# A fused attention and FFN kernel on one core: the last 1024 tokens of the FFN moved behind the attention heads and run 512 at a time

## The chip, the core and the metric

The kernel runs on one core of one Trainium2 chip. A core has five engines that work side by side and meet at semaphores: TensorE (PE; its weight loads are listed apart as PEld), VectorE (DVE), ScalarE (ACT), GpSimd (POOL) and SyncE (SP), which here issues all the transfers. The metric is the device time of one execution in microseconds (us), lower is better. Before the change it is 1208.37 us, the median of 3 runs (1208.25 to 1209.43).

## What is computed

64 attention heads (8 batches of 8 heads, 576 positions, 64 dimensions each) with a causal mask and a decay taken from cumulated logs of a forget gate; the results, laid side by side, are 4608 tokens of 512 features, and go through an FFN of 2048 hidden features with a leaky ReLU.

```python
scores = scale * np.matmul(q, k.transpose(0, 1, 3, 2))
cum = np.cumsum(np.log(np.clip(f, 0.0001, 1.0)), axis=-1)
scores = np.where(causal, -1000000000.0, scores + cum[:, :, :, None] - cum[:, :, None, :])
attn = np.exp(scores - np.max(scores, axis=-1, keepdims=True))
attn = attn / (np.sum(attn, axis=-1, keepdims=True) + 1e-09)
x = np.matmul(attn, v).transpose(0, 2, 1, 3).reshape(B * S, H * D)
h = x @ w_in                       # 4608 x 512 @ 512 x 2048
out = np.maximum(0.01 * h, h) @ w_out
```

All of it is in float32, and the FFN keeps the precision by splitting each operand into a high and a low part: every product is three matmuls (high by high, low by high, high by low).

## The kernel before

**Layout.** Attention of the first 256 positions of three batches is done first, by a simpler path (`early_scores`, `early_values`), while the FFN weights are loaded and split; they stay in SBUF for the rest of the program. Then come 64 *tasks*, one head each, in the batch order 0, 3, 4, 5, 6, 7, 1, 2. Tasks 8 to 47 are whole heads (576 rows); tasks 0 to 7 and 48 to 63 belong to the three batches whose first 256 rows are already done and have 320 rows.

**One head on the engines.** `scores(t, i)` makes row block i of the scores on PE (tiles `sc`, two PSUM buffers); DVE adds the mask and finds the maximum (line 437), ACT takes the exponential (line 443). One task later `transposes(t, i)` turns the block on PE (tiles `tr`), ACT and DVE copy it out as a high part `ph` and a low part `pl` (lines 487 and 489), and `values` multiplies both with v (`av`: first the matmuls that read `ph`, then those that read `pl`). There is one `ph` and one `pl` in SBUF. After every second head `inverse` turns the sums of the exponentials and sends them through DRAM, and `normalise` (line 584) multiplies and writes the pair's result to the DRAM array `xd` (line 587).

**The FFN as filling.** The generator `ffn()` goes over the 4608 tokens in 18 groups of T = 256. A group's tokens are read back from `xd` by one transfer of 512 KB (`fetch_group`, line 608) and split (`split_group`). For each p, a pair of blocks of 128 hidden features (8 pairs in all), the group has 24 matmuls that write `h` (12 for each half, 256 columns wide), a Prelu on ACT (`g`, line 654), the high part on DVE (`gh`, line 657), the low part on POOL or, after the last head, on DVE (`gl`, line 659), and one pair later 12 matmuls 512 columns wide that add to the two accumulators `o` (`second`). A *quantum* is one yield of the generator: 12 matmuls of `h` or 6 of `o`; a pair is 4 quanta and a group 32, so the FFN is 576. After the last pair ACT copies each accumulator to an `ost` tile (line 690, two buffers) and SP sends it to `out` (line 692).

**What sets the order.** In the main loop (lines 755 to 788) `fill(step)` stands between the parts of a head and adds `step` to a credit, nine times per head in all; each whole credit runs one quantum. Line 763 counts the quanta whose tokens are ready and not yet used, line 764 the heads to the end of the batch, and line 765 sets the step:

```python
have = ready[0] // T * NQ - used[0]
step = min(have / (left + SLACK), CAPS.get(t, MAXQ)) / 8
```

MAXQ is 9, so a head gets at most 9 x 9/8, about 10 quanta. Below, a head's *rate* is the value that line 765 divides by 8. The framework then orders the instructions on each engine by its own costs; on each engine they run strictly in that order. Following lines 763 to 765 by hand, the rate is 4.5 to 4.0 in tasks 0 to 7, 3.9 to 3.5 in 8 to 16, 6.7 down to 5.75 in 17 to 24, 7.4 to 6.5 in 25 to 32, 9.0 in 33 to 40, 8.8 to 7.75 in 41 to 48, 7.8 to 6.75 in 49 to 56 and 4.7 to 4.2 in 57 to 63. 500 quanta are used when the last head ends, and 76 run behind it.

## Time and profile before

| | |
|---|---|
| time, median of 3 runs | 1208.37 us (1208.25 to 1209.43) |
| the profiled execution | 1209.36 us, of which the profile's span is 1207.5 us |
| granted TensorE clock | 1.00 |
| PE busy | 1194.9 us, 99% of the span |
| DVE, ACT, POOL busy | 613.2, 633.2 and 460.8 us (51%, 52%, 38%) |
| FFN matmuls `h`, 128x256 | 3456, mean 283 to 286 ns each |
| FFN matmuls `o`, 128x512 | 1728, mean 395 to 402 ns each |

A row of a group or of the timeline gives the line of the program, the engine, the operation, output<-input by the program's names, and the shape. The duration of a matmul is from its start to its modelled end; since matmuls overlap in the array, the time one really takes is read from the spacing of starts, or from the chain of waits, which counts only what each adds. "Idle before" is the time for which the engine had nothing to do ahead of an instruction, with what ended it. In the trace the first score of task 8 starts at 228.1 us, that of task 17 at 333.8, of task 33 at 585.6, of task 48 at 872.3, of task 57 at 1011.6, and the last `av` of task 63 starts at 1093.85.

### The profile page before, as it was taken

The numbers are of one execution on the slowest core, as the hardware profiler recorded it, in microseconds if no ns is written. First come the engines' busy times: TensorE is split into PE (matmuls) and PEld (weight loads), VectorE is DVE, ScalarE is ACT, GpSimd is POOL, SyncE is SP. The second block draws the span as 40 slices with busy tenths as digits, with TensorE's granted clock in tenths as the row PEclk, the third lists the DMA queues.
The fourth block names the chain that finished last, engine by engine and source line by source line (L and its number), as shares of the span: only waits on it lengthen the run. The fifth ranks groups of instructions, "written<-read, shape, count | busy, mean of one in ns | idle before, by whom it ended". The sixth has DMA issues, their size and how long they took to land.

```text
span 1207.5 us, 22521 instructions
## 1 busy us (share of the span) xinstructions
PE 1194.9 (99%) x7828; PEld 1068.1 (88%) x7828; DVE 613.2 (51%) x1697; ACT 633.2 (52%) x1622; POOL 460.8 (38%) x473
## 2 busy tenths in 40 slices
PE   9999999999999999999999999999999999999998
PEld 6678888888899999999999999999999999998997
DVE  6888365566655555464544445444443434553221
ACT  5887465666755565555554545455444445552111
POOL 2000255555455445454435354444354543531000
PEclk9999999999999999999999999999999999999999
DMA  6565233334343233323332223232233223311000
GB/s 202 175 204 177 78 99 101 99 111 118 102 137 82 82 99 101 99 72 97 87 96 79 80 66 101 65 100 59 69 85 93 58 71 81 80 58 52 13 18 19
DMA packets 82130, 110.57 MB, mean 92 GB/s; under 512 B 20640, under 2 KB 51728, under 8 KB 82016
## 3 DMA queue, kind: packets, MB, share of 16 engines
q1 hardware_dynamic: 82016, 109.12, 31.2%
q8 instruction: 63, 1.03, 0.4%
q14 instruction: 51, 0.42, 0.1%
HBM read 65.32 MB, written 18.58 MB: 69 GB/s over the span
## 4 chain that ended last, share of the span: by engine, by line
PE 95%; DVE 2%; ACT 1%; DMA 1%; issue 1%; POOL 0%; SPq 0%; DVEq 0%; ACTq 0%; POOLq 0%
PE h L111 34%; PE o L111 33%; PE tr L115 8%; PE av L111 8%; PE sc L111 7%; PE sce L111 2%; PE ave L111 1%; PE ws L111 1%; PE warm L111 1%; PE tre L115 1%; DVE fixed_z L437 1%; DMA wraw<-in_w_in 0%; ACT g L654 0%; DVE pl L489 0%; DVE gh L657 0%
## 5 line engine op out<-in xcount | busy, mean ns | idle before, releaser
L659 POOL TENSOR_TENSOR gl<-g,gh 128x512 fp32r<-128x512 f32 x113 | 148.8, 1317 | 275.1 <-DVE gh L657 270.1
L111 PE MATMUL o<-wout_h,gh 128*128 128x512 f32 x576 | 231.3, 402 | 0.0
L111 PE MATMUL o<-wout_l,gh 128*128 128x512 f32 x576 | 227.4, 395 | 0.0
L111 PE MATMUL o<-wout_h,gl 128*128 128x512 f32 x576 | 227.1, 395 | 0.0
L443 ACT ACTIVATE fixed_z<-fixed_z,max 128x192 f32<-128x192 f32 (+3 forms) x272 | 161.0, 592 | 101.4 <-DVE max L437 99.1
L111 PE MATMUL h<-xh,win_h 128*128 128x256 f32 x1152 | 206.2, 286 | 0.0
L487 ACT CAST ph<-tr 128x192 fp32r<-128x192 f32 (+3 forms) x360 | 126.7, 373 | 148.5 <-PE tr L115 99.2
L111 PE MATMUL h<-xh,win_l 128*128 128x256 f32 x1152 | 200.3, 283 | 0.0
L437 DVE CUSTOM_DVE_ANT_0 fixed_z<-sc,tri 128x192 f32<-128x192 f32 (+3 forms) x272 | 122.4, 451 | 151.3 <-PE sc L111 148.4
L654 ACT ACTIVATE g<-h 128x512 f32<-128x512 f32 x144 | 85.8, 596 | 216.1 <-PE h L111 211.0
L657 DVE CAST gh<-g 128x512 fp32r<-128x512 f32 x144 | 72.4, 503 | 217.6 <-ACT g L654 215.9
L489 DVE TENSOR_TENSOR pl<-tr,ph 128x384 fp32r<-128x384 f32 (+3 forms) x296 | 137.3, 467 | 80.7 <-ACT ph L487 79.5
L111 PEld LDWEIGHTS h<-xh,win_h 128*128 128x128 f32 x1152 | 170.8, 190 | 5.8 <-issue 0.5
L111 PEld LDWEIGHTS h<-xh,win_l 128*128 128x128 f32 x1152 | 164.8, 190 | 0.5 <-issue 0.2
L111 PE MATMUL h<-xs,win_h 128*128 128x256 f32 x1024 | 164.4, 283 | 0.0
L115 PE MATMUL tr<-ident_r,fixed_z 128*128 128x128 f32 x888 | 145.3, 273 | 3.4 <-DVE ph L494 1.7
L111 PEld LDWEIGHTS h<-xs,win_h 128*128 128x128 f32 x1024 | 141.0, 191 | 0.0
L115 PEld LDWEIGHTS tr<-ident_r,fixed_z 128*128 128x128 f32 x888 | 107.6, 140 | 25.2 <-ACT rb L566 5.2
L111 PEld LDWEIGHTS o<-wout_h,gl 128*128 128x128 f32 x576 | 108.2, 188 | 24.4 <-DVE maxe L323 0.3
L111 PEld LDWEIGHTS o<-wout_l,gh 128*128 128x128 f32 x576 | 108.7, 189 | 16.0 <-issue 0.5
L111 PEld LDWEIGHTS o<-wout_h,gh 128*128 128x128 f32 x576 | 108.9, 189 | 14.8
L154 POOL TENSOR_TENSOR fixed_m2a<-raw,m 64x576 fp32r<-64x576 f32 x32 | 46.6, 1458 | 195.4 <-ACT m L399 173.8
(130 smaller groups left out, 1753.2 us busy)
## 6 DMA issues: line engine op xcount, KB each, us to landing
raw<-in_kT SPq DMA_DIRECT2D x64, 144.0 KB
m<-m SPq DMA_DIRECT2D x64, 144.0 KB
wraw<-in_w_in SPq DMA_DIRECT2D x16, 512.0 KB
wraw<-in_w_out SPq DMA_DIRECT2D x16, 512.0 KB
fixed_vm<-in_v SPq DMA_DIRECT2D x64, 128.0 KB
xs<-xd SPq DMA_DIRECT2D x16, 512.0 KB
out<-ost SPq DMA_DIRECT2D x28, 256.0 KB
raw<-in_qT SPq DMA_DIRECT2D x40, 144.0 KB
```

The costliest lines, as they stand in the source:

```text
L111: nc.tensor.matmul(*args, **kw)
L115: nc.tensor.transpose(*args)
L154: nc.gpsimd.tensor_tensor(out, a, b, op=ALU.subtract)
L437: nc.vector.tensor_tensor_reduce(out=z[:, a:b], in0=ps[:m, :b - a], in1=tri[:m, at:at + b - a], scale=-SCALE, scalar=3.0e38 if x == 0 else ...
L443: nc.scalar.activation(z, z, AF.Exp, bias=h["max"][:m, last:last + 1], scale=-1.0, accum_out=fixed["sum" + "ab"[s // 2 % 2]][:m, i, s % 2: ...
L487: nc.scalar.copy(strided(ph, run), source(ps, run))
L489: nc.vector.tensor_tensor(strided(pl, run), source(ps, run), strided(ph, run).bitcast(F32), op=ALU.subtract)
L654: nc.scalar.activation(g, ph, AF.Prelu, alpha=0.01)
L657: nc.vector.tensor_copy(gh, g)
L659: eng.tensor_tensor(gl, g, gh.bitcast(F32), op=ALU.subtract)
```

## The change

The generator's narrow groups end at the 14th; the last four (1024 tokens) become two *wide* groups of 512 tokens that run only when all heads are done. A wide group takes its hidden features 128 at a time: 12 matmuls 512 columns wide write one `h` bank (`hw`), Prelu, high and low part follow as before, and 12 matmuls go to four accumulators (`second_wide`, tiles `ow`). The four accumulators of the first wide group lie in the PSUM of `o0`, `o1` and `tr`, those of the second in `sc`, `o0` and `o1`. The tokens of the first wide group are fetched in one transfer of 1 MB into the SBUF of the heads' `ph`, with the high part in that of `pl` (`fetch_wide`, `split_wide`); those of the second use the narrow groups' buffers. All four accumulators of a wide group end together, pass through the same two `ost` buffers, and the very last one is copied by ACT and DVE, half each.

The planner counts no more than the 448 narrow quanta less LAST = 8, and from task 17 on the cap of the rate is 6.2 in place of 9, which makes about 7 quanta a head. By hand: tasks up to 16 keep their rate, 17 to 56 have 6.2 each, 57 to 63 have 3.9 to 3.4. 430 quanta are used when the last head ends, 18 narrow ones are left, and behind them the two wide groups.

```diff
--- before.py
+++ after.py
@@ -19,6 +19,9 @@
 HP = 4
 PARTS = (("part0", 1), ("part1", 1), ("ost", 2), ("ost", 2))
 MAXQ = 9
+LATEQ = 6.2
+LAST = 8
+WIDE = 2
 CAPS = {}
 SLACK = 3
 B2 = 5
@@ -618,7 +621,7 @@
         pending = None
         half = NFC // 2
         order = [(0, 0, HP), (1, 0, HP), (0, HP, half), (1, HP, half)]
-        order += [(n, 0, half) for n in range(2, NG)]
+        order += [(n, 0, half) for n in range(2, NG - 2 * WIDE)]
         for at, (n, p0, p1) in enumerate(order):
             while (n + 1) * T > ready[0]:
                 yield False
@@ -663,7 +666,92 @@
                 if p0 < p and at + 1 < len(order):
                     fetch_group(order[at + 1][0])
                 pending = (n, p, p0, p1, gh, gl, acc)
+        while not done:
+            yield False
+        for c in range(NCC):
+            split_wide(0, c)
         yield from second(*pending)
+        pending = None
+        for n in range(WIDE):
+            if n + 1 < WIDE:
+                fetch_wide(n + 1)
+            acc = [
+                psum.tile(
+                    [P, DM], F32, tag=tag, name=f"ow_{n}_{k}", bufs=1 if tag[0] == "o" else 2
+                ) for k, tag in enumerate(("sc", "sc", "o0", "o1") if n else ("o0", "o1", "tr", "tr"))
+            ]
+            for fc_ in range(NFC):
+                p, fs = fc_ // 2, slice(fc_ % 2 * P, fc_ % 2 * P + P)
+                ph = psum.tile([P, 512], F32, tag="h", name=f"hw_{n}_{fc_}")
+                terms = [
+                    (w, xx, c) for w, xx in ((win_h[p], 1), (win_l[p], 1), (win_h[p], 0))
+                    for c in range(NCC)
+                ]
+                for y, (w, xx, c) in enumerate(terms):
+                    matmul(
+                        ph, w[:, c, fs], wide[n][xx][c], start=y == 0, stop=y == len(terms) - 1
+                    )
+                g = one.tile([P, 512], F32, tag="b2", name=f"gw_{n}_{fc_}", bufs=B2)
+                nc.scalar.activation(g, ph, AF.Prelu, alpha=0.01)
+                gh = one.tile([P, 512], F32R, tag="b2", name=f"ghw_{n}_{fc_}", bufs=B2)
+                gl = one.tile([P, 512], F32R, tag="b2", name=f"glw_{n}_{fc_}", bufs=B2)
+                nc.vector.tensor_copy(gh, g)
+                nc.vector.tensor_tensor(gl, g, gh.bitcast(F32), op=ALU.subtract)
+                yield True
+                if pending is not None:
+                    second_wide(*pending)
+                    yield True
+                pending = n, fc_, gh, gl, acc
+                if n + 1 < WIDE and 8 <= fc_ < 8 + NCC:
+                    split_wide(n + 1, fc_ - 8)
+        second_wide(*pending)
+        yield True
+
+    wide = {}
+
+    def fetch_wide(n):
+        xs = wide[n] = []
+        for name in ("xl", "xh"):
+            xs.append([])
+            for x in range(n + 1):
+                y = one.tile(
+                    [P, NCC // (n + 1), 512], F32R, tag="b4" if n else {"xl": "ph", "xh": "pl"}[name],
+                    name=f"{name}w_{n}_{x}", bufs=B4 if n else 1,
+                )
+                xs[-1] += [y[:, c] for c in range(NCC // (n + 1))]
+                if name == "xl":
+                    at = NTOK - 512 * (WIDE - n)
+                    cs = slice(x * 2 * P, x * 2 * P + NCC // (n + 1) * P)
+                    nc.sync.dma_start(
+                        y.bitcast(F32), xd[cs, at:at + 512].rearrange("(c p) t -> p c t", p=P)
+                    )
+
+    def split_wide(n, c):
+        xl, xh = (x[c] for x in wide[n])
+        nc.scalar.copy(xh, xl.bitcast(F32))
+        nc.vector.tensor_tensor(xl, xl.bitcast(F32), xh.bitcast(F32), op=ALU.subtract)
+
+    def second_wide(n, fc_, gh, gl, acc):
+        p, e = fc_ // 2, fc_ % 2
+        for k in range(4):
+            ts = slice(k * P, (k + 1) * P)
+            for x, (gg, w) in enumerate(((gh, wout_h[p]), (gh, wout_l[p]), (gl, wout_h[p]))):
+                matmul(
+                    acc[k], gg[:, ts], w[:, e, :],
+                    start=(fc_ == 0 and x == 0), stop=(fc_ == NFC - 1 and x == 2),
+                )
+            if fc_ < NFC - 1:
+                continue
+            o = one.tile([P, DM], F32, tag="ost", name=f"ostw_{n}_{k}", bufs=2)
+            mine = [(slice(0, DM), nc.scalar.copy)]
+            if n == WIDE - 1 and k == 3:
+                mine = [
+                    (slice(0, DM // 2), nc.scalar.copy), (slice(DM // 2, DM), nc.vector.tensor_copy)
+                ]
+            for c, copy in mine:
+                copy(o[:, c], acc[k][:, c])
+                for x, row, m in segments((NTOK - 512 * (WIDE - n)) // P + k):
+                    nc.sync.dma_start(out[row:row + m, c], o[x:x + m, c])
 
     def second(n, p, p0, p1, gh, gl, acc):
         for k in range(T // P):
@@ -760,9 +848,9 @@
             load_v(t + 1)
         before = list(range(max(tasks[t - 1][1] - 1, 0), NCH)) if t else []
         now = list(range(*tasks[t][1:])) if t < nt else []
-        have = ready[0] // T * NQ - used[0]
+        have = min(ready[0] // T * NQ, (NG - 2 * WIDE) * NQ - LAST) - used[0]
         left = min((e + 2 - t for e in ends if e + 1 >= t), default=1)
-        step = min(have / (left + SLACK), CAPS.get(t, MAXQ)) / 8
+        step = min(have / (left + SLACK), CAPS.get(t, MAXQ if t < 17 else LATEQ)) / 8
         fill(step)
         for i in range(5):
             if i in before:
@@ -787,6 +875,7 @@
             split_v(t + 1)
         fill(step * (3 - len(spans(t - 1)) if t else 1))
     done.append(nt)
+    fetch_wide(0)
     for _ in range(NG * NQ):
         fill(1)
 
```

Three places show what this does to the engines' order. The first is PE at the end of task 40, a whole head of the stretch whose cap falls from 9 to 6.2; `tr_40_4` is the last transpose, `sc_41_4` the next head's last scores, `o_...` and `h_...` are FFN quanta. Before:

```order
L115 MATMUL tr_40_4_9089<-ident_r_94,fixed_z4_1671 128x128 x4
L111 MATMUL sc_41_4_0_9096<-m1_41_8943,s1_41_8942 128x288
L111 MATMUL sc_41_4_0_9096<-fixed_m2b_177,fixed_s2b_174 128x288
L111 MATMUL sc_41_4_1_9100<-m1_41_8943,s1_41_8942 128x288
L111 MATMUL sc_41_4_1_9100<-fixed_m2b_177,fixed_s2b_174 128x288
L111 MATMUL o_10_0_0_9106<-wout_h_0_116,gh_10_0_8988 128x512
L111 MATMUL o_10_0_0_9106<-wout_l_0_124,gh_10_0_8988 128x512
L111 MATMUL o_10_0_0_9106<-wout_h_0_116,gl_10_0_8989 128x512
L111 MATMUL o_10_0_0_9106<-wout_h_0_116,gh_10_0_8988 128x512
L111 MATMUL o_10_0_0_9106<-wout_l_0_124,gh_10_0_8988 128x512
L111 MATMUL o_10_0_0_9106<-wout_h_0_116,gl_10_0_8989 128x512
L111 MATMUL av_40_0_9114<-ph_40_8992,fixed_vs_1673 128x448 x2
```

After:

```order
L118 MATMUL tr_40_4_8701<-ident_r_94,fixed_z4_1671 128x128 x4
L114 MATMUL sc_41_4_0_8708<-m1_41_8579,s1_41_8578 128x288
L114 MATMUL sc_41_4_0_8708<-fixed_m2b_177,fixed_s2b_174 128x288
L114 MATMUL sc_41_4_1_8712<-m1_41_8579,s1_41_8578 128x288
L114 MATMUL sc_41_4_1_8712<-fixed_m2b_177,fixed_s2b_174 128x288
L114 MATMUL h_9_1_8731<-xh_9_8165,win_h_1_101 128x256 x2
L114 MATMUL av_40_0_8719<-ph_40_8616,fixed_vs_1673 128x448 x2
L114 MATMUL av_40_0_8719<-ph_40_8616,fixed_vs_1673 128x320
L114 MATMUL av_40_0_8719<-ph_40_8616,fixed_vs_1673 128x192
L114 MATMUL av_40_0_8719<-ph_40_8616,fixed_vs_1673 128x64
L114 MATMUL av_40_0_8719<-pl_40_8617,fixed_vs_1673 128x448 x2
```

Between the last transpose of the head and the first `av` that reads its `ph` stood four score matmuls and six FFN matmuls; now there are the four and two narrow ones. The same four and two stand there in tasks 36 to 44; in the other tasks from 17 to 47 it is as before.

The second place is ACT from the last head's last copy on (`x_62` is the last pair's result, `g_15_5` the Prelu of pair 5 of group 15, `xhw_0` the high part of the first wide group, `xhw_1` that of the second). Before:

```order
L548 COPY x_62_13065<-av_63_0_13174 64x320
L654 ACTIVATE g_15_5_13201<-h_15_5_13161 128x512
L654 ACTIVATE g_15_6_13249<-h_15_6_13221 128x512
L654 ACTIVATE g_15_7_13292<-h_15_7_13267 128x512
L654 ACTIVATE g_16_0_13335<-h_16_0_13310 128x512
L690 COPY ost_15_0_13347<-o_15_0_0_12807 128x512
```

After:

```order
L551 COPY x_62_12301<-av_63_0_12397 64x320
L657 ACTIVATE g_13_4_12446<-h_13_4_12421 128x512
L731 CAST xhw_0_0_12420<-xlw_0_0_12418 128x512 x4
L657 ACTIVATE g_13_5_12489<-h_13_5_12464 128x512
L657 ACTIVATE g_13_6_12532<-h_13_6_12507 128x512
L731 CAST xhw_1_0_12624<-xlw_1_0_12620 128x512
L657 ACTIVATE g_13_7_12575<-h_13_7_12550 128x512
L731 CAST xhw_1_0_12624<-xlw_1_0_12620 128x512
L731 CAST xhw_1_1_12625<-xlw_1_1_12622 128x512 x2
L778 COPY ost_13_0_12607<-o_13_0_0_12155 128x512
L778 COPY ost_13_1_12617<-o_13_1_0_12191 128x512
```

Four copies that need the 1 MB transfer have come between the Prelus of pairs 4 and 5, and four more stand around that of pair 7. On DVE the four subtractions that go with them stand between `gl` of pair 4 and `gh` of pair 5. On SP the transfer itself stands right behind the write of the last pair's result to `xd`.

The third is ACT at the very end. Before:

```order
L654 ACTIVATE g_17_5_13916<-h_17_5_13891 128x512
L654 ACTIVATE g_17_6_13959<-h_17_6_13934 128x512
L654 ACTIVATE g_17_7_14002<-h_17_7_13977 128x512
L690 COPY ost_17_0_14026<-o_17_0_0_13748 128x512
L690 COPY ost_17_1_14035<-o_17_1_0_13755 128x512
```

After:

```order
L695 ACTIVATE gw_1_14_13585<-hw_1_14_13572 128x512
L695 ACTIVATE gw_1_15_13616<-hw_1_15_13603 128x512
L752 COPY ostw_1_0_13637<-ow_1_0_13122 128x512
L752 COPY ostw_1_1_13643<-ow_1_1_13123 128x512
L752 COPY ostw_1_2_13650<-ow_1_2_13124 128x512
L752 COPY ostw_1_3_13656<-ow_1_3_13125 128x256
```

Two evictions have become four, and the last is of half the width; the third uses the buffer of the first, and the fourth that of the second, so each has to wait until the transfer out of its buffer has landed.

## The prediction

> **What bounds the kernel now.** I read the busy times and the chain of waits first.
>
> ```profile
> PE 1194.9 (99%) x7828; PEld 1068.1 (88%) x7828; DVE 613.2 (51%) x1697; ACT 633.2 (52%) x1622; POOL 460.8 (38%) x473
> ...
> PE 95%; DVE 2%; ACT 1%; DMA 1%; issue 1%; POOL 0%; SPq 0%; DVEq 0%; ACTq 0%; POOLq 0%
> ```
>
> PE carries 95% of the chain that ended last. No other engine is over 52% busy, so time changes only where PE has to do less, or waits more. The next view is the busy time of the engines by stretch: tasks 8 to 16 (whole heads, rate 3.9 to 3.5), 17 to 32 (7.4 to 5.75), 33 to 47 (9.0 to 8.0), and FFN alone behind the heads. The columns are start:end, length, and busy time and count for PE, PEld, DVE, ACT and POOL.
>
> ```profile
> 228.10:333.80 105.70, 101.89 (x687) 91.83 (x686) 65.08 (x207) 72.31 (x203) 54.43 (x56) 1.00 0.40 110
> 333.80:585.60 251.80, 251.70 (x1700) 230.91 (x1698) 137.55 (x387) 142.41 (x382) 119.81 (x116) 1.00 0.33 94
> 585.60:872.30 286.70, 286.70 (x1931) 263.92 (x1929) 131.01 (x375) 142.27 (x372) 127.57 (x119) 1.00 0.29 82
> ...
> 1105.07:1195.42 90.35, 90.35 (x578) 82.07 (x578) 21.24 (x35) 11.90 (x20) 4.69 (x2) 1.00 0.06 18
> ```
>
> PE idles only in the first of these stretches, where the heads have least FFN to fill with. From task 33 on a head runs as densely as the bare FFN. So the FFN that the change takes out of the heads isn't congested there, and moving it gains nothing by itself; it can only leave holes. What a hole costs I read from the waits of the weight loads, which show a stall sooner than the overlapping matmuls: who waited for whom, us in total, times, longest. Tasks 8 to 16, the three largest:
>
> ```profile
> PEld tr L115 <- ACT rb L566: 3.3, 5, 0.8
> PEld av L111 <- DVE pl L489: 1.4, 3, 0.8
> PEld av L111 <- ACT ph L487: 1.1, 3, 0.5
> ```
>
> Tasks 17 to 32, all that there is:
>
> ```profile
> PEld av L111 <- ACT ph L487: 0.6, 2, 0.4
> PEld sc L111 <- DVE max L437: 0.4, 1, 0.4
> PEld tr L115 <- ACT rb L566: 0.3, 1, 0.3
> ```
>
> Tasks 57 to 63, the three largest:
>
> ```profile
> PEld tr L115 <- ACT rb L566: 0.9, 3, 0.5
> PEld av L111 <- ACT ph L487: 0.6, 2, 0.4
> PEld sc L111 <- DVE max L437: 0.4, 1, 0.4
> ```
>
> That is 5.8 us over 9 heads (0.64 each) at rates under 4, 1.3 us over 16 (0.08 each) at 5.75 to 7.4, and 1.9 us over 7 (0.27 each) of the shorter heads at 4.2 to 4.7.
>
> **The change part by part.** *The wide matmuls.* The chain behind the heads shows what the two shapes take when nothing else is there.
>
> ```profile
> 1105.07 2.87 PE h L111 x24
> 1107.94 2.77 PE o L111 x12
> ```
>
> 24 matmuls of 256 columns take 2.87 us (119.6 ns each), 12 of 512 take 2.77 (231 ns each). The change turns the first into a second 2.77, for 4 groups of 8 pairs: 32 x 0.10 = **-3.2 us**, if a wide `h` costs what an `o` costs (same width, new weights for each). Bounds: nothing, if it costs two narrow ones, to -3.4, from the rounding of the two rows. [...]
>
> *Whole heads with fewer quanta.* Tasks 17 to 32 had rates between 5.75 and 7.4 and now have an even 6.2. Their waits are all in single heads, where few FFN matmuls stand between the last transpose and `av`; with the even rate this doesn't occur before task 36. I take -0.9 of their 1.3 us (bounds -1.3 and 0). Tasks 33 to 47 had 9.0 to 8.0 and now have 6.2. In tasks 36 to 44 PE's order now has four score matmuls and two narrow `h` (about 4 x 0.13 + 2 x 0.12 = 0.77 us) ahead of the first `av`, where it had 1.9 us. The same tight place stands in the trace at task 29:
>
> ```profile
> 546.20 0.40 PE L111 MATMUL o<-wout_h,gh 128*128 128x512 f32 x1
> 546.62 0.96 PE L111 MATMUL av<-ph,fixed_vs 128*128 128x448 f32 x5
> 547.58 0.92 PE L111 MATMUL av<-pl,fixed_vs 128*128 128x448 f32 x4
> ```
>
> An `o` takes 0.23 us, so the `av` came 0.19 us late, and the `pl` half starts 0.96 us behind it, while the five matmuls ahead of it have 1472 columns, 0.66 us at 231/512 ns each, a little more with what each takes beside: another 0.2 us, 0.4 together. With nine such heads that is 3.6 us at most; no wait at all is the other bound (of four tight places in tasks 17 to 32 the waits above show two, with 0.6 us). I take 0.25 each, **+2.2 us**. Late behind it is the next head's `tr`, since `ph` is one tile; it keeps its 1.9 us of FFN.
>
> *Shorter heads.* Tasks 49 to 56 had 7.8 to 6.75 and now 6.2, in the band of 0.08 us a head, nothing to count. Tasks 57 to 63 had 4.7 to 4.2 and now 3.9 to 3.4. From about 6.5 to about 3.7 a whole head's waits rose from 0.08 to 0.64, 0.2 us for each step of 1 in the rate; 0.8 less on top of 0.27 makes 0.43, and since waits that the three rows leave out come on top I take +0.2 a head, **+1.4 us** (bounds 0 and, if each head waits 0.5 more, +3.5).
>
> *The handover.* ACT stands still at the four copies until the 1 MB has landed, and behind them the Prelu of pair 5 is held, then `gh` and `gl` on DVE, then PE's `o` of pair 5. The rows of the last head and of the fetch behind it:
>
> ```profile
> 1093.85 0.74 PE L111 MATMUL av<-ph,fixed_vs 128*128 128x320 f32 x5
> ...
> 1095.03 0.66 PE L111 MATMUL h<-xh,win_h 128*128 128x256 f32 x4
> ...
> 1096.80 0.35 SPq L587 DMA_DIRECT2D xd<-x  x1
> 1100.50 7.37 SPq L608 DMA_DIRECT2D xs<-xd  x2
> ...
> 1104.07 0.69 DVE L613 CAST xh<-xs 128x1024 fp32r<-128x1024 f32 x1 [5.54 <-DMA xs<-xd]
> ...
> 1199.01 0.43 DVE L657 CAST gh<-g 128x512 fp32r<-128x512 f32 x1 [4.42 <-ACT g L654]
> 1199.54 0.69 DVE L659 TENSOR_TENSOR gl<-g,gh 128x512 fp32r<-128x512 f32 x1
> ```
>
> Counted from the first `av`: the pair's write goes out at 2.95, the 1 MB behind it at 3.3. Half a megabyte took 1104.07 - 1100.50 = 3.6 us to land, so the whole takes 3.6 to 7.2 and is there at 6.9 to 10.5. The four subtractions on DVE (0.69 each, the first 0.6 behind the landing), `gh` and `gl` end 4.5 us later, at 11.4 to 15.0. PE meanwhile has `av` (1.18), two `o` (0.46), and `h` and `o` in turn, 2.87 + 2.77 + 2.87 + 2.77 + 2.87: it wants `gh` at 15.8. So the wait is covered, with 0.8 us left at the worst. A little is late at the end of group 13: the copies and subtractions around pair 7 (0.59 + 0.60 + 0.43 + 2 x 0.69 and the handings on, about 3.4 us from the end of `h`) meet 2.77 + 0.46 of cover. **+0.3 us**, bounds 0 and +2.5. The second wide group's transfers and splits lie inside the first's 16 blocks of 5.5 us.
>
> *The end.* Rows of the last eviction, and SP's wait for what it sent:
>
> ```profile
> 1203.11 1.74 SPq L692 DMA_DIRECT2D out<-ost  x2
> ...
> 1203.47 0.40 PE L111 MATMUL o<-wout_h,gl 128*128 128x512 f32 x1
> ...
> 1203.90 0.58 ACT L690 COPY ost<-o 128x512 f32<-128x512 f32 x1 [0.82 <-PE o L111]
> ...
> SPq L822 <- DMA out<-ost: 1.6, 2, 1.4
> ```
>
> PE ends at 1203.87; the last transfer is issued from 1204.51 to 1204.85, SP waits 1.6 more, so it lands 2.0 us after its issue, 2.65 after PE. Now the accumulators follow each other every 0.69 us. The second ends 1.39 before PE's end, its copy 0.8 before, its second piece is issued at -0.4 and lands at +1.65; only then can the fourth be copied (about 0.4 for a half), issued twice (0.4 to the second) and landed (2.0): +4.4 against 2.65, **+1.7 us**. Lower bound 1.3, if a half lands 0.4 sooner. The write to `xd` took 1100.50 - 1096.80 = 3.7 to be waited out; with that for the first landing it is 3.4.
>
> **The sum.** -3.2 - 0.9 + 2.2 + 1.4 + 0.3 + 1.7 = +1.5 us. The profiled execution took 1209.36 us, its span 1207.5 and 1.9 around it, 1.0 above the median of 1208.37; it would become 1210.9, and the median **1209.9**.
>
> **The rivals.** *The heads starve* (slower). Waits grow as in tasks 8 to 16: all nine tight heads pay 0.4 (+3.6), tasks 57 to 63 pay 0.5 more each (+3.5), nothing comes back in 17 to 32. -3.2 + 3.6 + 3.5 + 0.3 + 1.7 = +5.9: 1214.3. It decides from about 0.08 us per head over tasks 17 to 63: the other terms make -1.2, so 3.6 us of new waits are the 2.4 that can be told. For it: 0.64 us a head at the rates where tasks 57 to 63 now go. Against it: 0.08 at rates around 6.2.
>
> *The heads lose nothing.* The tight places are met by their 0.77 us, and the end is cheap: -3.4 - 1.3 + 1.3 = -3.4, 1205.0. For it: no wait at all in tasks 33 to 47, and only 0.6 us in two of four tight places before. Against it: the row at 546.62.
>
> *A wide `h` costs two narrow ones.* What a matmul takes beyond its columns then grows with them, and +3.2 comes back: 1213.1. For it: an `h` has 12 matmuls in one bank and reads activations where `o` reads weights. Against it: nothing in the rows of `o` tells the two apart. [...]
>
> *The transfer is late.* If 1 MB takes 11 us, `gh` comes 3 us after PE wants it: 1212.9. It decides from 8 us of landing. Against it: the 3.6 us for half of it, with the queue empty.
>
> **How the numbers follow.** Forecast 0.53, starving 0.20, nothing lost 0.13, wide costs more 0.08, late transfer 0.06. This kernel's measurement can tell 0.2%, 2.4 us, from no change. Nearly all of "nothing lost" is faster by that: 0.11. Slower are most of starving, wide and late (0.31) and the forecast's upper edge (0.07): 0.38. The rest, 0.51, is within. The forecast's own range is 1207.4 to 1212.4 from the bounds of the heads and the end; 8 times in 10 it should lie in 1205.5 to 1213.8, which takes in most of both sides.
>
> **What would show it.** Right: behind the heads blocks of 2.77 and 2.77 us in the chain; `av` of tasks 36 to 44 with waits for `ph` and `pl` of 0.2 to 0.4 us; ACT idle before the first copy of `xhw_0`, ended by the transfer, with no gap of PE there; the last eviction waiting for `out<-ostw`, and some 4.4 us from PE's end to the last landing. Wrong: PE idle in tasks 17 to 35, a block of 2.87 for the wide `h`, or a hole of PE behind the 1 MB.

## The result, and the profile after

The changed kernel takes **1216.38 us** (median of 5 runs, 1215.76 to 1217.08) against 1208.37 us for the kernel before (now 5 runs, among them the three above, 1208.03 to 1209.43). The ratio is 1.0067, with a 95% interval of 1.0055 to 1.0078: slower by two thirds of a per cent. 1209.9 had been predicted, with 1205.5 to 1213.8 as the range, so the prediction was wrong, by 6.5 us. The profiled execution took 1216.33 us, its span is 1214.5 us, 7.0 more than before. From here on lines are those of the changed kernel, whose file is longer (`tr` is L118, `rb` L569, the copies `ph` and `pl` L490 and L492).

The page still shows TensorE as the bound, at 99%, with 384 matmuls fewer:

```profile
PE 1196.7 (99%) x7444; PEld 1047.6 (86%) x7444; DVE 624.6 (51%) x1720; ACT 635.2 (52%) x1630; POOL 429.0 (35%) x451
...
PE 94%; DVE 2%; ACT 2%; issue 1%; DMA 1%; POOL 1%; SPq 0%; ACTq 0%; DVEq 0%; POOLq 0%
```

Busy time hides what happened; the stretches show it. Tasks 17 to 32, 33 to 47 and 48 to 56 of the changed kernel (columns as in the prediction):

```profile
332.50:576.90 244.40, 240.62 (x1628) 220.45 (x1625) 132.24 (x385) 140.50 (x380) 120.02 (x114) 1.00 0.34 96
576.90:805.50 228.60, 228.49 (x1541) 208.77 (x1539) 127.51 (x364) 132.79 (x359) 110.22 (x107) 1.00 0.34 95
805.50:929.40 123.90, 123.76 (x828) 112.57 (x826) 57.79 (x162) 63.66 (x160) 57.49 (x63) 1.00 0.30 85
```

PE stands still for 244.40 - 240.62 = 3.8 us in tasks 17 to 32, where it stood for 0.1 in 251.8 before. Shorter waits hardly show as idle, since matmuls overlap (behind the heads an `h` starts every 119.6 ns, and its record lasts 278 to 283) and the modelled end of one covers a short wait of the next. So I also use a **loss** of each head: the time from its first score matmul to the next head's, less what the matmuls between take at the spacing of starts that they have where nothing waits (119.6 ns for an `h`, 231 for an `o`, 109 for a transpose, 204 for a score or `av` of 448 columns, and so on). What this counting can't see leaves a floor of 0.40 to 0.45 us for a whole head. The stretch of a task holds the scores of its own head and the transposes and `av` of the head before. By it:

| tasks | before | after | difference | predicted |
|---|---|---|---|---|
| 17 to 32 | 8.6 | 12.5 | **+3.9** | -0.9 |
| 33 to 47 | 6.6 | 9.2 | +2.6 | +2.2 |
| 48 to 56 | 1.3 | 2.8 | +1.5 | 0 |
| 57 to 62 | 2.8 | 3.1 | +0.4 | +1.4 (57 to 63) |

Within tasks 17 to 32 the loss alternates. Two neighbours, each with 7 quanta:

```profile
530.68:546.37 15.69, 15.16 (x108) 14.00 (x107) 9.24 (x24) 8.87 (x24) 6.82 (x7) 1.00 0.28 78
546.37:561.23 14.86, 14.86 (x108) 13.95 (x106) 6.84 (x24) 8.02 (x22) 6.91 (x8) 1.00 0.29 81
```

The first is task 30 and loses 1.12 us, the second is task 31 and loses 0.40, the floor. So it alternates from 18 to 32. The long ones are those in which the transposes of an odd head run, behind which `inverse` sends the reciprocals of a pair through a transpose of their own, `rt`. The waits of tasks 17 to 32, TensorE's two largest and one of another kind:

```profile
PEld tr L118 <- ACT rb L569: 5.5, 8, 0.8
...
PE tr L118 <- DVE ph L497: 2.3, 5, 0.5
...
PEld h L114 <- POOL xs L157: 0.8, 1, 0.8
```

The last is a single wait in task 18 for the tokens of a group, `xs`, which POOL splits. It isn't the hole at `rt`: it also stands in e5 below, where no transpose of these tasks waits. Counted by the spacing of starts, the +3.9 of tasks 17 to 32 is +4.4 ahead of transposes in the even tasks, +0.8 for `xs`, and -1.3 for waits of before that are gone.

The timeline of the hole in task 30 (start, length, engine, operation, and in brackets the idle time before it and what ended it):

```profile
532.43 0.60 PE L118 MATMUL tr<-ident_r,fixed_z 128*128 128x128 f32 x4
...
533.07 0.44 ACT L490 CAST ph<-tr 128x64 fp32r<-128x64 f32 x2 [1.25 <-PE tr L118]
533.07 0.27 PE L118 MATMUL rt<-ident_r,r 128*10 128x128 f32 x1
...
533.38 0.25 ACT L569 COPY rb<-rt 10x128 f32<-10x128 f32 x1
533.47 0.28 PE L114 MATMUL h<-xh,win_h 128*128 128x256 f32 x1
533.53 0.36 DVE L492 TENSOR_TENSOR pl<-tr,ph 128x192 fp32r<-128x192 f32 x1 [1.80 <-ACT ph L490]
...
533.90 0.23 DVE L497 TENSOR_TENSOR ph<-tr,ph 64x64 fp32r<-64x64 f32 x1
...
534.27 0.41 PE L118 MATMUL tr<-ident_r,fixed_z 128*128 128x128 f32 x2 [0.53 <-DVE ph L497]
```

The tiles `tr`, `rt` and `av` take turns in two PSUM buffers. The second transposes took one at 532.43, `rt` took the other at 533.07, so the third transposes need the first one back, and it is free only when its last copy ends at 534.13. Between stand the scores and one narrow `h`: the third of the nine places for quanta in a head is empty (in tasks 18 to 22 the fourth, with the same effect), and at the even rate it stays empty head after head.

In tasks 37 to 45, where the `av` of heads 36 to 44 run, the loss comes ahead of `av`, as worked out: 2.1 us more than before. The other 0.5 of tasks 33 to 47 stand ahead of scores in 46 and 47. TensorE's largest wait of tasks 33 to 47:

```profile
PEld av L114 <- ACT ph L490: 1.4, 5, 0.4
```

Behind the heads there is no hole at the handover. A narrow and two wide pieces of the chain:

```profile
1016.38 2.87 PE h L114 x24
1019.25 2.77 PE o L114 x12
...
1030.48 5.58 PE hw L114 x24
...
1105.94 2.80 PE hw L114 x12
1108.74 2.80 PE ow L114 x12
...
1142.11 2.80 PE ow L114 x12
1144.90 2.76 PE hw L114 x12
```

PE runs from 1030.48 to 1208.78, 178.3 us; 32 narrow blocks of 2.87 + 2.77 would be 180.5. The wide form saves **2.2 us**, not 3.2. The end, with the two `ost` buffers:

```profile
1206.73 1.28 ACT L752 COPY ostw<-ow 128x512 f32<-128x512 f32 x2 [2.85 <-PE ow L114]
...
1207.34 4.87 SPq L754 DMA_DIRECT2D out<-ostw  x6
...
1209.46 0.59 ACT L752 COPY ostw<-ow 128x512 f32<-128x512 f32 x1 [1.46 <-DMA out<-ostw]
1211.00 0.37 ACT L752 COPY ostw<-ow 128x256 f32<-128x256 f32 x1 [0.95 <-DMA out<-ostw]
1211.41 0.42 DVE L752 COPY ostw<-ow 128x256 f32<-128x256 f32 x1 [6.27 <-ACT ostw L752]
```

Two copies wait for a store to land, as predicted; the second of them starts 2.2 us behind PE's end (1208.78 to 1211.00). DVE's half of the last one comes behind ACT's, not beside it. From the start of the last matmul to the end of the span it takes 6.16 us in place of 4.03: **+2.1**. All together: +3.9 + 2.6 + 1.5 + 0.4 - 2.2 + 2.1 = +8.3, of which 1.3 is missing in the profiled pair only because task 17 starts 1.3 us sooner in the one of after, behind a program that is the same up to there.

### The profile page after: what moved, and what is told of

Read it like the earlier page. It is cut to its first block, busy times and chain, and to the rows that moved or that the text cites. A ratio compares the mean times of both kernels' runs of the same rounds, so it can differ in the third digit from the quotient of the medians.

```text
span 1214.5 us, 21783 instructions
## 1 busy us (share of the span) xinstructions
PE 1196.7 (99%) x7444; PEld 1047.6 (86%) x7444; DVE 624.6 (51%) x1720; ACT 635.2 (52%) x1630; POOL 429.0 (35%) x451
## 4 chain that ended last, share of the span: by engine, by line
PE 94%; DVE 2%; ACT 2%; issue 1%; DMA 1%; POOL 1%; SPq 0%; ACTq 0%; DVEq 0%; POOLq 0%
PE h L114 26%; PE o L114 25%; PE av L114 8%; PE tr L118 8%; PE hw L114 7%; PE ow L114 7%; PE sc L114 7%; PE sce L114 2%; PE ave L114 1%; PE ws L114 1%; PE warm L114 1%; PE tre L118 1%; ACT g L657 1%; DVE fixed_z L440 1%; DVE pl L492 1%
## 5 line engine op out<-in xcount | busy, mean ns | idle before, releaser
L490 ACT CAST ph<-tr 128x192 fp32r<-128x192 f32 (+3 forms) x360 | 126.7, 373 | 145.7 <-PE tr L118 87.4
L114 PE MATMUL o<-wout_h,gh 128*128 128x512 f32 x448 | 180.6, 403 | 0.0
L114 PE MATMUL o<-wout_l,gh 128*128 128x512 f32 x448 | 177.4, 396 | 0.0
L114 PE MATMUL o<-wout_h,gl 128*128 128x512 f32 x448 | 176.7, 396 | 0.0
L492 DVE TENSOR_TENSOR pl<-tr,ph 128x384 fp32r<-128x384 f32 (+3 forms) x296 | 137.1, 467 | 71.0 <-ACT ph L490 69.7
L114 PE MATMUL h<-xh,win_h 128*128 128x256 f32 x896 | 165.9, 287 | 0.0
L114 PE MATMUL h<-xh,win_l 128*128 128x256 f32 x896 | 159.2, 282 | 0.0
L118 PE MATMUL tr<-ident_r,fixed_z 128*128 128x128 f32 x888 | 146.3, 274 | 6.6 <-DVE ph L497 4.0
L114 PEld LDWEIGHTS h<-xh,win_h 128*128 128x128 f32 x896 | 134.3, 190 | 4.4 <-issue 0.5
L118 PEld LDWEIGHTS tr<-ident_r,fixed_z 128*128 128x128 f32 x888 | 106.9, 140 | 29.5 <-ACT rb L569 10.6
L114 PEld LDWEIGHTS h<-xh,win_l 128*128 128x128 f32 x896 | 129.7, 190 | 0.5 <-issue 0.2
L114 PE MATMUL h<-xs,win_h 128*128 128x256 f32 x768 | 123.4, 283 | 0.6 <-POOL xs L157 0.6
L114 PE MATMUL sc<-m,s 128*128 128x288 f32 (+1 forms) x336 | 121.0, 365 | 0.4
L114 PEld LDWEIGHTS h<-xs,win_h 128*128 128x128 f32 x768 | 105.7, 191 | 0.8 <-POOL xs L157 0.8
```

Source lines behind the costliest of these rows:

```text
L114: nc.tensor.matmul(*args, **kw)
L118: nc.tensor.transpose(*args)
L490: nc.scalar.copy(strided(ph, run), source(ps, run))
L492: nc.vector.tensor_tensor(strided(pl, run), source(ps, run), strided(ph, run).bitcast(F32), op=ALU.subtract)
```

## The experiments

The theory that the trace suggests, **places**: a quantum is worth what it hides at its place, and the even rate keeps the same two of nine places empty for many heads in a row. The rivals: **amount** (fewer quanta in a head cost time wherever they stand), and **tail** (the wide part and its end cost it). The median of the kernel before was 1208.1 to 1208.8 in the four sets of runs; ratios are to it.

### Heads and tail apart

The cap without the wide part, and the wide part (of one group) without the cap:

```diff
 # e7_cap_alone, from the kernel before
-        have = ready[0] // T * NQ - used[0]
+        have = min(ready[0] // T * NQ, (NG - 4) * NQ - 8) - used[0]
...
-        step = min(have / (left + SLACK), CAPS.get(t, MAXQ)) / 8
+        step = min(have / (left + SLACK), CAPS.get(t, MAXQ if t < 17 else 6.2)) / 8
 # e8_wide_alone, from the changed kernel
-LATEQ = 6.2
+LATEQ = MAXQ
...
-WIDE = 2
+WIDE = 1
...
-        have = min(ready[0] // T * NQ, (NG - 2 * WIDE) * NQ - LAST) - used[0]
+        have = ready[0] // T * NQ - used[0]
```

> The kernel before with the cap of 6.2 from task 17 on and the limit that keeps 72 quanta behind the heads, and nothing else: all groups narrow to the end, 8 pairs of 24 and 12 matmuls each. The heads' program on TensorE is that of the changed kernel, instruction for instruction. Theory 'places' (and 'amount'): the heads lose what they lose in the changed kernel, 27.6 us in tasks 17 to 62 against 19.2; 1208.1 + 8.4 = 1216.5 (1215.5 to 1217). Rival 'tail': 1208 to 1209, since the tail is that of before.

Measured: 1216.96 us, ratio 1.0070 (1.0057 to 1.0083). Tasks 17 to 62 lose 27.9 us, and the same stretch idles:

```profile
331.80:576.60 244.80, 240.75 (x1629) 220.57 (x1627) 135.49 (x385) 140.53 (x380) 120.10 (x115) 1.00 0.34 96
```

> The changed kernel with the rates of before (no cap, no limit) and one wide group in place of two, the last 512 tokens: the heads' program on TensorE is that of before, instruction for instruction, and half of the wide saving is kept, with the whole of the changed end and a handover by which the first and only wide group is fetched behind the heads. Theory 'places' (heads cost, the tail is about even): wide -1.1 (16 blocks of 5.575 for 5.645), end +2.1, handover 0 to 0.5: 1209.1 to 1209.8. Rival 'tail': 1212 or more.

Measured: 1209.91 us, ratio 1.0009 (1.0001 to 1.0018); heads 17 to 62 lose 19.3 us as before, the end takes 6.19 us. So the whole slowdown is in the heads: one wide group with its end costs 1.1 us, and the changed kernel's two are 0.6 below e7 with the same heads, both about what can be told. "Tail" falls.

### The same quanta at other places

Four kernels differ from each other in one number. Each gives every head from task 17 to 55 exactly 7 quanta; the credit at task 17 decides which two of the nine places stay empty.

```diff
 # e1_places_clear (e2: 0.14, e3: 0.59, e5: 0.36), from the changed kernel
-LATEQ = 6.2
+LATEQ = 56 / 9
...
         step = min(have / (left + SLACK), CAPS.get(t, MAXQ if t < 17 else LATEQ)) / 8
+        if t == 17:
+            credit[0] = 0.92
```

Counted in the order of the code, the first place is ahead of the first transposes, the second to sixth follow the five parts of transposes and scores (`rt` comes behind the third), the seventh and eighth the two parts of `av`, and the ninth ends the head. Empty are the fifth and ninth in e1, the first and sixth in e2, the third and eighth in e3, the second and seventh in e5; where the expectations describe a place otherwise, this holds.

> From task 17 on every head gets exactly 7 quanta at its nine places (rate 56/9 in place of 6.2, so 7.00 in place of 6.975 a head), and the credit is set once, at task 17, so that the two empty places of each head are the third behind the transposes and the last, in tasks 17 to 55: neither the one ahead of the reciprocals' transpose rt nor the one ahead of av. Everything else is the changed kernel. Theory 'places' (the changed kernel's 8 us in tasks 17 to 56 come from where the two empty places fall): those heads go back to their floor, 0.40 to 0.45 us each for whole heads; tasks 17 to 32 lose 7.0 in place of 12.5 us, 33 to 47 lose 6.6 in place of 9.15, 48 to 56 1.3 to 2; the time is 1207.5 to 1209.5. Rival 'amount' (fewer quanta in a head leave less to hide behind, wherever they stand): within 1 us of the changed kernel's 1216.4. Rival 'tail' (the cost is in the wide part and the end): the same 1216.4.

> The same 7.00 quanta a head, with the credit set so that the empty places of tasks 17 to 55 are the first and the one ahead of av. Theory 'places': the av waits for ph and pl in all of these heads, 0.15 to 0.5 us each as in tasks 37 to 46 of the changed kernel (mean 0.25), so 39 x 0.25 = 8 to 10 us above the kernel with the clear places: 1216 to 1219; no hole ahead of a tr in tasks 18 to 32. Rivals 'amount' and 'tail': the same time as the kernel with the clear places.

> The same 7.00 quanta a head, with the credit set so that the empty places of tasks 17 to 55 are the third, which stands between rt and the next head's tr, and the one before the last tr. Theory 'places': every head behind an odd one (18, 20, ... 56) has a hole of 0.55 to 0.7 us ahead of a tr, ended by the copies of the tr tile before rt or by rb; 16 heads x 0.6 among the whole ones and 0.2 to 0.4 for each of the 4 shorter ones, 10 to 12 us above the kernel with the clear places: 1218 to 1221. The odd ones stay at 0.40 to 0.45. Rivals 'amount' and 'tail': the same time as the kernel with the clear places.

| empty places | time | ratio (95%) | loss 17-32 | 33-47 | 48-56 |
|---|---|---|---|---|---|
| e1: 5th, 9th | 1214.41 | 1.0053 (1.0040 to 1.0065) | 10.0 | 9.4 | 2.8 |
| e2: 1st, 6th | 1220.18 | 1.0103 (1.0089 to 1.0116) | 12.7 | 10.6 | 3.9 |
| e3: 3rd, 8th | 1217.97 | 1.0086 (1.0072 to 1.0099) | 12.9 | 10.9 | 1.9 |
| e5: 2nd, 7th | 1208.73 | 1.0000 (0.9991 to 1.0009) | 8.0 | 6.3 | 1.4 |

By the spacing of starts these sums hold single waits that don't recur from head to head: the one for `xs` in task 18 (0.9 us in e3, 1.4 in e5), and 1.0 in task 18 of e2, behind a copy on DVE that took 4.02 us. Without them tasks 17 to 32 lose 10.0, 11.7, 12.0 and 6.6 us.

The first three differ, as the theory has it, but not as expected. e2 and e3 are 5.8 and 3.6 us above e1, where 8 to 10 and 10 to 12 had been expected, so their order is the other way round; and e1 is 2 us below the changed kernel, not 7 to 9. At 7 quanta "amount" would still do for a good part of that. The waits of tasks 17 to 32 show what had been left out; e1, e2 and e3:

```profile
PEld sc L114 <- DVE max L440: 1.7, 4, 0.4
```
```profile
PEld av L114 <- ACT ph L490: 2.8, 9, 0.4
```
```profile
PEld tr L118 <- ACT rb L569: 5.9, 8, 0.8
...
PE tr L118 <- DVE ph L497: 3.8, 8, 0.5
```

Each pair has its own wait. In e2 it is `av`, in e3 `rt` (20, 22 and so on to 46, in which an odd head's transposes run, lose 1.01 to 1.12 us each, the others 0.41). In e1 it is a third: with the fifth place empty the last scores come straight behind those before them, and their two PSUM buffers are held until DVE has the maxima. So the theory has three kinds of place, and e5 tests it where all three are filled.

> The kernel with the clear places, with the credit set at task 17 to 0.36 in place of 0.92: again 7.00 quanta a head, now with the second place (ahead of the first transposes) and the one between the two parts of av empty in tasks 17 to 55. With 0.92 every head lost 0.1 to 0.35 us at a place that had not been counted: the last four score matmuls come straight behind the ones before, and wait for DVE's max of the same PSUM buffers. Tasks 33 to 36 of the changed kernel stand by chance at the places of this run and lose 0.39 to 0.44 each, the floor. Theory 'places', with all three kinds of place counted: tasks 17 to 32 lose 6.7 to 7.0 us, 33 to 47 6.3 to 6.5, 48 to 56 1.3 to 2.0; 1207.5 to 1209.5. Rival 'amount' (two empty places cost about 0.2 us a head wherever they are): the 1214.4 of the kernel with 0.92, 10 and 9.4 us.

Measured: 1208.73 us, 7.7 less than the changed kernel with the same wide part, the same end and the same quanta. 29 of the 31 heads from 17 to 47 lose 0.39 to 0.44 us, the floor, and in tasks 17 to 32 the only wait of a weight load that the trace lists is the one for `xs` in task 18:

```profile
PEld h L114 <- POOL xs L157: 1.3, 1, 1.3
```

"Amount" falls at this rate: with 7 quanta each these whole heads lose less (14.3 us) than in the kernel before (15.2), which gives most of them more, at rates of 5.75 to 9. e2 and e3 are 11.5 and 9.2 us above e5.

### rt by itself

```diff
 # e11_rt_later, from the changed kernel
-            if i == 1 and t and tasks[t - 1][0] % 2:
+            if i == (2 if 17 < t < 34 else 1) and t and tasks[t - 1][0] % 2:
```

> The changed kernel with every quantum where it is; only the reciprocals and their transpose rt, in tasks 18 to 33, come one part later (behind the third transposes and scores, ahead of the fourth). Theory 'rt' (the holes of tasks 18 to 32 come about because rt takes one of the two tr buffers, and with the third place empty the next two transposes wait for copies of the tiles ahead of it): holes of 0.45 to 0.69 us vanish from tasks 24 to 32, and 0.1 to 0.4 stays in 18 to 22, whose fourth place is the empty one; tasks 17 to 32 lose 8.5 to 9.7 us in place of 12.5, nothing else changes: 1212.5 to 1213.5. Rival: the transposes there wait for exp or for the engines behind, whatever rt does: 1216.4.

Measured: 1215.61 us, ratio 1.0059 (1.0045 to 1.0073); tasks 17 to 32 lose 10.7 us in place of 12.5, the rest of the heads as before. The kind is right, the size only half: 24, 26 and so on to 32 still wait 0.30 to 0.38 us. The waits now name `rt` and DVE's subtraction:

```profile
PEld tr L118 <- PE rt L118: 2.5, 5, 0.6
...
PE tr L118 <- DVE pl L492: 0.5, 3, 0.2
```

Wherever `rt` stands, it takes one of the two buffers, and the transposes behind it need the copies of those ahead of it. No run gave `rt` a buffer of its own. 0.8 us of this run's time against the changed kernel is also about what two sets of runs differ by; the trace carries the verdict.

### The end

```diff
 # e4_four_buffers, from the changed kernel
-            o = one.tile([P, DM], F32, tag="ost", name=f"ostw_{n}_{k}", bufs=2)
+            tag, m = PARTS[k ^ 2]
+            o = one.tile([P, DM], F32, tag=tag, name=f"ostw_{n}_{k}", bufs=m)
 # e6_free_end, from e5_places_free; the last copy is whole on ACT in both;
 # e9_end_again also has the four buffers, and the last block two accumulators
 # behind the one before it
...
-        second_wide(*pending)
+        for k in range(4):
+            second_wide(*last, (k,))
+            second_wide(*pending, (k,))
```

> The changed kernel, with the four output tiles of a wide group in four buffers (the last two in the buffers of the partial outputs, free by then) in place of two. Theory 'buffers': the last copy needn't wait for the second output to land; from the start of the last matmul to the end of the span it takes 4.0 to 4.4 us as in the kernel before in place of 6.1: 1214.0 to 1214.7. If the two halves of the last copy, or the last transfer itself, were what takes the time, nothing changes: 1216.4.

Measured: 1216.04 us, ratio 1.0068 (1.0055 to 1.0080): no change. In the profiled execution, the slowest of the five at 1218.14 us, the copies no longer wait, but one of SP's issues takes 1.83 us, where the least took 0.33, and the end is 6.37 us:

```profile
1211.47 1.83 SPq L755 DMA_DIRECT2D out<-ostw  x1
```

> The kernel before in this list, with another end: the last two blocks of the second product run accumulator by accumulator (12 matmuls... six for each of the two, one accumulator behind the other), so that the accumulators end 1.39 us apart as in the kernel before and not 0.69, and the last one is copied whole on ACT. Theory 'spacing' (copies and transfers of 256 KB come too close for two buffers and for SP, which with four buffers took 1.8 us to issue one of them): from the start of the last matmul to the end of the span 4.0 to 4.3 us in place of 6.1, so 1.8 to 2.1 us less: 1205.5 to 1207.5. Rival (the end is bound by the landing of the last megabyte whatever its spacing): no change.

> The kernel with the free places and the spaced end, with two more edits at the end. There the end took 4.86 us, 1.30 less than 6.16 and not 1.8 to 2.1, for two reasons that the trace shows: the second product of the last pair's half came one accumulator behind that of the one before, so TensorE waited 0.39 us for gh and gl; and the last copy waited 0.8 us for the second output's store to land. Now the last block comes two units of three matmuls behind (0.69 us more cover), and the four outputs have four buffers. Theory 'spacing': no hole of TensorE in the last 24 matmuls (5.36 us from the first to the last start in place of 5.75), and 4.0 to 4.2 us from the start of the last one to the end: 1.0 to 1.3 us less, 1207.1 to 1207.5. Rival: SP issues the last stores late, as with four buffers before (one issue of 1.8 us), and the end takes 4.8 or more.

Measured: e6 1208.41 us (0.9999, 0.9990 to 1.0008), e9 1208.22 us (0.9996, 0.9988 to 1.0005). The ends take 4.86 and 4.35 us in place of 6.16, so spacing the accumulators and copying the last one whole on ACT do together what four buffers alone didn't; what each is worth was not tested. But the last block now comes too soon for its own high and low parts; from the first to the last start of the last 24 matmuls it takes 5.75 us in both where it took 5.35. In e9:

```profile
1197.62 0.19 PEld L114 LDWEIGHTS ow<-wout_h,ghw 128*128 128x128 f32 x1 [0.23 <-DVE ghw L698]
...
1198.42 0.19 PEld L114 LDWEIGHTS ow<-wout_h,glw 128*128 128x128 f32 x1 [0.50 <-DVE glw L699]
```

My expectation that two accumulators of cover would do was wrong; 0.9 and 1.4 us of the 2.1 are won back, and in the medians that can't be told from nothing.

### The heads that were sparse all along

Tasks 9 to 16 are the same before and after and have four or five quanta for nine places. If places decide, they can be moved there too.

```diff
 # e10_sparse_heads, from e9; put() replaces the nine calls of fill(step)
+    def put(t, at, step):
+        if 9 <= t < 17:
+            credit[0] = 0.0
+            step = float(at[0] in ((0, 2, 4, 7), (0, 2, 3, 7))[t % 2 == 0])
+        fill(step)
+        at[0] += 1
 # e12_sparse_same
-            step = float(at[0] in ((0, 2, 4, 7), (0, 2, 3, 7))[t % 2 == 0])
+            step = float(at[0] in (0, 2, 3, 7))
```

> The kernel of the run before, and in tasks 9 to 16, which get only four quanta for nine places (34 in all before, 32 now), the quanta stand at fixed places: the first, the third, the eighth, and the fourth where the head ahead is odd (its rt takes a tr buffer there), the fifth where it is even. These heads are the same in the kernel before and in the changed one and lose 11.0 us together with task 8. Theory 'places': what a head loses is set by which places are empty, not by how many: 0.45 to 0.75 us for each of tasks 10 to 16 in place of 1.38 (8 to 16 lose 5.5 to 7.5 in place of 11.0), so 3.5 to 5.5 us less than the run before: 1202 to 1204, faster than the kernel before by 0.35 to 0.5%. Rival 'amount': with four quanta a head has too little to hide behind; 10 to 11 us as before, 1207.3.

Measured: 1206.26 us, ratio 0.9980 (0.9972 to 0.9989), 2.0 less than e9 where 3.5 to 5.5 were expected. Tasks 8 to 16 lose 10.8 us, hardly less than 11.0: 12, 14 and 16 fell from 1.4 to 0.76 each, but 13 and 15 rose from 0.73 and 0.82 to 1.39 and 1.38, and a new hole of 1.9 us stands in task 10. Their sum is what "amount" foretold; only the single heads speak for the places, and the next run tests them. The gain came from elsewhere, 1.4 us of it because the wait for `xs` in task 18 is gone, so tasks 17 to 32 are at 6.6.

> The run before (quanta of tasks 9 to 16 at fixed places), with the first, third, fourth and eighth place in every one of these heads, in place of the fifth for every second. There the heads at this set lost 0.75 each (12, 14, 16) and those at the other 1.38 (11, 13, 15), both with four quanta. Theory 'places': all go to about 0.75, tasks 11 to 16 lose 4.5 in place of 6.4 us; if the single hole of 1.9 us in task 10 (DVE's copy of g took 2.1 us beside POOL's subtraction) also doesn't recur, 8 to 16 lose 7.0 to 7.5 in place of 10.8: 1202.5 to 1204.5. Rival 'amount': heads 11, 13 and 15 stay at 1.38, since each has four quanta as before, 1206.3.

Measured: **1204.69 us, ratio 0.9969 (0.9957 to 0.9981)**. 11, 13 and 15 went to 0.85, with the same four quanta; the hole in task 10 stayed, so 8 to 16 lose 9.3 and not 7.0 to 7.5. So the places count here too, but with four quanta none of the sets that were tried brings a head to the floor of 0.40. This kernel beats the one before by 0.3% and the changed one by 11.7 us.

## Why the prediction was wrong

**The step that failed** is the term of tasks 17 to 32, "I take -0.9 of their 1.3 us (bounds -1.3 and 0)". It measured +3.9, outside its bounds. The reason given for it, "with the even rate this doesn't occur before task 36", held: no `av` waits before task 37, and 1.3 us of the waits of before are gone. But the step had looked for one tight place only, the last transposes to `av`, and so put new waits at all other places at nothing, where +4.4 us came ahead of transposes and +0.8 in the single wait for `xs`. It did not count the work between one use of a PSUM buffer and the next: `rt` puts one more tile into the same two buffers, and with the place beside it empty the copies, which in the hole above end 1.1 us behind the last transpose (533.03 to 534.13), had only the scores and one narrow `h` to lie behind. The row was there to be seen: "PEld tr <- ACT rb" is the largest wait of tasks 8 to 16, and I read it as a price of a low rate, not as the price of one empty place. Nor does anything in the prediction tell the phases of the credit apart: e5, at nearly the same rate, takes 1208.73 us, 1.2 below the forecast. The term is 4.8 of the 6.8 us by which the terms were off; "PE idle in tasks 17 to 35" was named as what would show it wrong.

**Tasks 48 to 56**, "in the band of 0.08 us a head, nothing to count", measured +1.5: the same error, with the last scores behind DVE's maxima and `rt` as the places (50 and 54 lose 0.24 us each ahead of a score). **Tasks 57 to 63** were taken at +1.4, by the slope of waits against the rate, and tasks 57 to 62 measured +0.4; e5 and e12 show that such a slope is no property of the rate alone.

**Tasks 33 to 47** were right: +2.2 was predicted for nine heads ahead of `av`, and 2.1 came there; 0.5 more, ahead of scores in tasks 46 and 47, had not been foreseen. **The handover** was right: no hole.

**The wide matmuls** were taken at -3.2 and measured -2.2, within the bounds: the wide `hw` of the second group costs 2.76 and the first group's 2.80, and `ow` 2.80 where `o` costs 2.77. **The end**, +1.7, measured +2.1. What was short is the landing of the second output: it lets the last copy start 2.2 us behind PE's end, where 1.65 had been taken. That the two halves of that copy came one behind the other cost little, since their issues, 0.46 us apart, had been taken 0.4 apart in any case.

**The rival "heads starve"**, 1214.3, came nearest by luck, by a mechanism that the runs refute: it charged the tight heads 0.4 each and the shorter heads the rest, and let nothing come back in tasks 17 to 32; the shorter heads lost next to nothing, and 17 to 32 was where the cost was.

## What to carry to other kernels

Filling work that is dealt out at an even rate falls into a fixed pattern: with a rate near a whole number of pieces a head, the same places stay empty for dozens of heads, and which ones they are can be worth more (here some 11 us between the best and the worst of four phases) than how many. Before such a rate is changed, list for every place what must finish behind it: not only the operand of the next step, but each PSUM buffer's next use, and every tile that shares it, a small one such as `rt` too. Waits that grow as filling gets rarer are no slope to extrapolate; look at which place is empty where they stand.

## What the runs showed of the hardware

A **DVE copy beside a POOL subtraction** can take five times as long and more. In e10 it made the hole of task 10:

```profile
256.17 2.37 POOL L157 TENSOR_TENSOR xs<-xs,xh 128x1024 fp32r<-128x1024 f32 x1 [2.72 <-issue]
...
256.73 2.10 DVE L660 CAST gh<-g 128x512 fp32r<-128x512 f32 x1 [0.69 <-ACT g L657]
...
258.74 0.61 DVE L440 CUSTOM_DVE_ANT_0 fixed_z<-sc,tri 128x448 f32<-128x448 f32 x1
...
259.42 0.40 PE L114 MATMUL sc<-m,s 128*128 128x288 f32 x1 [1.75 <-DVE max L440]
```

The same copy takes 0.43 us alone; here it begins 0.56 us into POOL's instruction and ends 0.29 behind it, the maxima behind it are late, and PE waits 1.75. Of the changed kernel's 112 copies `gh`, the 76 that overlap with no POOL instruction take 0.36 to 0.43 us and the six that begin ahead of one 0.41 to 0.42; of the 30 that begin inside one, 11 take 0.41 to 0.44, and the other 19 take 0.50 to 1.36 and end 0.28 to 0.29 us behind it. In e10, of the copies `gh` that overlap with POOL, the eleven that begin ahead of POOL's instruction take 0.41 to 0.43 us, and of the eleven that begin inside one nine take 0.46 to 2.10. What holds the copy back, no run tells. In task 17 of e2 the copy takes 4.02 us: two POOL subtractions follow each other there, and it ends 0.28 us behind the second. A second such hole, of 1.1 us, stands in task 39 of e10, where DVE's multiplication of 64 columns took 3.80 us (0.90 at the median in the changed kernel). The kernel before has a copy of 2.07 us too, at 346.96, and no hole behind it; why the holes come where they do was not tested.

**One issue on SP's queue can take five times as long as another.** In e4 the fifth of the last six stores took 1.83 us to issue, against 0.33 at the least. It came 2.5 us behind the first; but in e9 five stores issued within 3.5 us took 0.6 at most, and the kernel before has single issues of up to 2.39 us in the heads. So it isn't shown that the short distance of the stores did it, and what the issue waits for, no run tells.

**Matmuls of 512 columns cost 229.5 to 233.4 ns by starts** inside a block of 12, at a granted clock of 1.00 throughout: 233.4 in the whole first wide group but for its start, in the second 229.5 for `hw` and 233.0 for `ow`, 231.6 for the narrow `o`. The operands' layout differs between them; no run took it apart, so what moves the cost, by less than 1 us in all here, stays open.
